# Final layer's outputs packed dense, with 3 tiles' grace and half pace, and an unread matmul in each poor tile

## The chip, the cores and the metric

The kernel runs on one core of a Trainium2 chip, in one launch. The metric is the device time of that launch in microseconds. TensorE (PE) multiplies, ScalarE (ACT) computes the exponentials, VectorE (DVE) copies, masks, normalizes and adds, GpSimd (POOL) and SyncE (SP) mostly issue DMAs. TensorE's clock is granted by a throttle; the profile lists what share of full speed was granted at each moment.

## The reference

Four attention layers with residuals: A, B, A, B. x has 2048 rows of 640, there are 32 heads of 20.

```python
def A(x, wqkv, wo):               # B is the same without the mask
    q, k, v = split(x @ wqkv)     # 32 heads, Dh = 20
    s = einsum("bhqd,bhkd->bhqk", q, k) * Dh ** -0.5
    s = where((i - j >= 0) & (i - j < 256), s, -1e9)
    return merge(softmax(s) @ v) @ wo
x = x + A(layernorm(x), A_wqkv, A_wo)
x = x + B(layernorm(x), B_wqkv, B_wo)
x = x + A(layernorm(x), A_wqkv, A_wo)
x = x + B(layernorm(x), B_wqkv, B_wo)
```

## The kernel before

**Layers, chunks, groups, units.** The layers are numbered 0 to 3; 0 and 2 have a window of 256 keys, 1 and 3 see all keys. The queries are cut into four chunks c of 512 columns, the heads into eight groups g of four. One (layer, chunk, group) is a unit; in layers 1 and 3 chunk 0 is cut further by keys (`PARTS`). The list `units` fixes the order of all units and weaves units of a windowed layer between units of a full one. The last units are those of layer 3, chunks 1 to 3, with nothing woven between.

**Tiles of the main loop.** The loop near the end of the kernel runs over tiles t. A tile is three score banks (two or four in some cases) of one unit: scores of one head for 128 keys by 512 queries, one PSUM bank each. The scores of a tile go into banks 0 to 2 for even t and 3 to 6 for odd t (`sp`), so that ACT can take the exponentials of one tile (L1284, tile `pt`) while PE writes the scores of the next (L1253). After the scores of tile t the loop calls `load_ahead()` (loads of later units on SP), `pump()` (background work, up to a credit) and `keep_clock()`, and then emits values times exponentials of an earlier tile into bank 7 (L1317). Scores use 32 rows of the array and values 21 of its columns for each head, so that four heads' matmuls run side by side.

**Order.** All of it stands under a manual schedule: each engine runs its instructions in exactly the order in which the Python code emits them. Engines wait for each other through semaphores only.

**Background tasks.** Layernorm and its transposes (`t_ln`), projections (`t_block`, `t_v`), the normalizing of a finished unit (`t_tail`) and the output projection (`t_out`) are generators. A `yield ("hold", n)` or `("pe", n)` takes n from the credit and lets the loop go on; `("wait", n)` puts the task to sleep for n tiles. `rate(t)` says how much credit a tile brings; for the tiles of layer 3, chunks 1 to 3 (`t >= len(tiles)`) it is 0.9. `take_m()` hands out one of two spare banks (5 and 6), and after an early stage bank 6 alone; `drop_m()` gives it back, from the next tile on.

**Normalizing and output.** When a unit ends, `t_tail` inverts the sums of the exponentials (L1020 to L1039), spreads them over the partitions (L1048) and multiplies (L1052) into `on[:, g, :]`. There the 80 values of a group lie as four strips of 20 rows at partitions 0, 32, 64 and 96; the other rows meet zero rows of `wop`, the output weights laid out in the same way. `t_out` therefore runs 8 matmuls over g (L541) for each of 4 x 2 blocks of 128 queries by 320 outputs, and adds the residual on DVE (L550). For the very last chunk `t_before_last` does groups 0 to 5 early (L572), and the end is left with groups 6 and 7. `load_wop` fetches the weights (four DMAs of 20 partitions, L132) whenever the next output projection belongs to the other weight matrix.

**Unread matmuls.** `unread(b)` (L620) multiplies the identity by the masks into a spare bank; nobody reads the result. `state["heat"]` counts the background and unread matmuls of a tile in units of one unread matmul, `state["carry"]` (up to 3) what earlier tiles had beyond their need, and `state["least"]` what a tile has to have: 1.76 for a tile of three banks from layer 1's first unit on, 0 from layer 3, chunk 1 on. `cool()` says that heat and carry fall short, and `keep_clock()` then first takes background work, if the credit is above -0.5, and else an unread matmul. If no spare bank is free in this tile, it stops there:

```python
            b = min(mfree, key=mfree.get)
            if mfree[b][0] > state["tick"]:
                break
            unread(b)
```

Of the kernel before, what the change touches and what calls it, by code (L numbers as in the profile page):

```python
# [12 lines left out]
ALU = mybir.AluOpType  # L13
ACT = mybir.ActivationFunctionType

P = 128
# [3 lines left out]
DH = 20  # L20
NT = S // P
KD = D // P
G = 8
C = 512
NC = S // C
EPS = 1e-5
SCALE = DH ** -0.5
HD = D // 2
# [21 lines left out]
def kernel(  # L50
# [75 lines left out]
        nc.sync.dma_start(out=x_sb[:, 4 * c : 4 * c + 4, :], in_=xin[:, 4 * c : 4 * c + 4, :])  # L126
    nc.sync.dma_start(out=wv_sb[1][:], in_=wq_view[1][:, :, 2 * D : 3 * D])

    def load_wop(w):
        v = wo_in[w].rearrange("(g j e) f -> j e g f", g=G, j=4)  # L130
        for j in range(4):
            nc.sync.dma_start(out=wop[32 * j : 32 * j + DH, :, :], in_=v[j])  # L132
# [41 lines left out]
    ready = set()  # L174
    todo = []
    tails = []
    state = {"tick": 0, "held": None, "credit": 0.0, "early": True, "act": True, "unit": 0, "heat": 0.0, "carry": 0.0, "least": 0.0}

    class Task:

# [348 lines left out]
    def t_out(l, c):  # L529
        on = ons[l, c]  # L530
        last = (l, c) == (3, NC - 1)
        while last and "before_last" not in ready:
            yield ("wait", 1)
        assert out_seq[out_n[0]] == l % 2
        for qb in range(4):
            for i in range(2):
                mb = yield from take_m()
                yp = ps[:, mb, 0:HD]
                g0 = G - 2 if last else 0
                for g in range(g0, G):  # L540
                    nc.tensor.matmul(  # L541
                        yp, lhsT=on[:, g, qb * P : (qb + 1) * P],
                        rhs=wop[:, g, i * HD : (i + 1) * HD],
                        start=(g == g0), stop=(g == G - 1),
                    )
                    if g < G - 1:
                        yield ("hold", 0.14)
                xv = x_sb[:, 4 * c + qb, i * HD : (i + 1) * HD]
                had = part_o["t"][:, 2 * qb + i, 0:HD] if last else xv
                nc.vector.tensor_tensor(out=xv, in0=had, in1=yp, op=ALU.add)  # L550
                drop_m(mb)
                yield ("pe", 0.14)
            if l < 3:
                stats(l + 1, c, qb)
            else:
                nc.sync.dma_start(out=xout[:, 4 * c + qb, :], in_=x_sb[:, 4 * c + qb, :])
        ons.pop((l, c))
        ready.add(("out", l, c))
        ready.add(("x", l + 1, c))
        n = out_n[0] = out_n[0] + 1  # L560
        if n < len(out_seq) and out_seq[n] != out_seq[n - 1]:
            load_wop(out_seq[n])

    def t_before_last():

        on = ons[3, NC - 1]
        for qb in range(4):
            for i in range(2):
                mb = yield from take_m()
                yp = ps[:, mb, 0:HD]  # L570
                for g in range(G - 2):
                    nc.tensor.matmul(  # L572
                        yp, lhsT=on[:, g, qb * P : (qb + 1) * P],
                        rhs=wop[:, g, i * HD : (i + 1) * HD],
                        start=(g == 0), stop=(g == G - 3),
                    )
                    if g < G - 3:
                        yield ("hold", 0.14)
                xv = x_sb[:, 4 * (NC - 1) + qb, i * HD : (i + 1) * HD]
                nc.vector.tensor_tensor(  # L580
                    out=part_o["t"][:, 2 * qb + i, 0:HD], in0=xv, in1=yp, op=ALU.add
                )
                drop_m(mb)
                yield ("pe", 0.14)
        ready.add("before_last")
# [27 lines left out]

    def cool():

        return state["heat"] + state["carry"] < state["least"]

    def unread(b):
# [13 lines left out]
    def keep_clock():  # L632

        while cool():
            t = choose(False)
            if t is not None and state["credit"] > -0.5:
                state["credit"] -= advance(t)
                continue
            b = min(mfree, key=mfree.get)
            if mfree[b][0] > state["tick"]:  # L640
                break
            unread(b)
        spare = state["heat"] + state["carry"] - state["least"]
        state["carry"] = min(max(spare, 0.0), 3.0)
        state["heat"] = 0.0
# [360 lines left out]
    def t_tail(l, c, g, on, oT):  # L1006
        def fill(count):

            for n in range(count * ((l, c, g) == (3, NC - 1, G - 1))):
                nc.tensor.matmul(  # L1010
                    ps[:, 0, :], lhsT=ident[:], rhs=masks[:, 0, :], start=True, stop=True
                )

        yield ("wait", 2)
        fill(2)
        mb = yield from take_m()
        warm_bank(mb)
        zp = ps[:, mb, 0:16]
        for qb in range(4):
            nc.tensor.matmul(  # L1020
                zp[:, 4 * qb : 4 * qb + 4], lhsT=oT[:, qb * P : (qb + 1) * P],
                rhs=sel4[:], start=True, stop=True,
            )
        rz = rzp.tile([P, 16], F32, name="rz", tag="rz")
        nc.vector.reciprocal(out=rz[:], in_=zp)  # L1025
        drop_m(mb)

        hl = rzp.tile([P, 2, 16], BF16, name="hl", tag="hl")
        nc.vector.tensor_copy(out=hl[:, 0, :], in_=rz[:])
        nc.vector.tensor_tensor(out=hl[:, 1, :], in0=rz[:], in1=hl[:, 0, :], op=ALU.subtract)  # L1030
        yield ("pe", 0.25)
        fill(3)
        yield ("wait", 2)
        mb = yield from take_m()
        warm_bank(mb)
        rp = ps[0:32, mb, :].bitcast(BF16)[:, 0:P]
        nc.tensor.transpose(out=rp, in_=hl[:].rearrange("p n r -> p (n r)"), identity=ident[:])
        rT = rzp.tile([32, P], BF16, name="rT", tag="rT")
        nc.vector.tensor_copy(out=rT[:], in_=rp)  # L1039
        drop_m(mb)  # L1040
        yield ("pe", 0.1)
        fill(1)
        yield ("wait", 2 if state["tick"] < last_tick[0] else 1)
        mb = yield from take_m()
        warm_bank(mb)
        zb = ps[:, mb, :]
        for qb in range(4):
            nc.tensor.matmul(  # L1048
                zb[:, qb * P : (qb + 1) * P], lhsT=spread4[:, qb, :], rhs=rT[:],
                start=True, stop=True,  # L1050
            )
        nc.vector.tensor_tensor(out=on[:, g, :], in0=oT[:], in1=zb, op=ALU.mult)  # L1052
        drop_m(mb)
        yield ("pe", 0.3)
        fill(3)
        ready.add(("tail", l, c, g))
        if (l, c, g) == (3, NC - 1, G - 3):
            push("before_last", t_before_last(), 0, 8.0)
        if g == G - 1:
            need = first_use(l + 1, c, 0) if l < 3 else len(units) + c  # L1060
            push(("out", l, c), t_out(l, c), need, 9.0)
            if l < 3:
                push_layer(l + 1, c)
    def t_zeros():

        z = ka_all[:, G : G + 4, :].rearrange("p a b -> p (a b)")
        yield ("wait", 4)
        for n in range(2):
            nc.gpsimd.dma_start(
                out=wop[:, 4 * n : 4 * n + 3, :].rearrange("p g f -> p (g f)"), in_=z[:, 0 : 3 * D]  # L1070
            )
            nc.gpsimd.dma_start(out=wop[:, 4 * n + 3, :], in_=z[:, 0:D])
            yield ("wait", 1)
        load_wop(0)
        for t in (*kts, *qts):
            nc.gpsimd.dma_start(out=t[:], in_=z[:, 0 : t.shape[1]])
            yield ("wait", 1)
        ready.add("kts")
# [67 lines left out]
    with tc.manual_schedule():  # L1146
# [49 lines left out]
        def rate(t):  # L1196

            if t >= len(tiles):
                return 0.9
            u = tiles[t][0][0]  # L1200
            if index[u.l, u.c, u.g, u.part] < woven:
                return 1.2
            done, r = 0.0, 0.6 if state["early"] else 0.3
            for task in todo:
                done += max(task.left, 0.0)
                if task.need < len(units):
                    r = max(r, done / max(starts[id(units[task.need])] - t - 16, 1))
            return min(1.1 * r, 1.0 if u.l == 0 else 0.9)
# [10 lines left out]
        while ended is None or t < ended + 8:  # L1219
# [3 lines left out]
            if t < len(tiles) or banks:  # L1223
# [23 lines left out]
                if n_b == 4:  # L1247
                    mseq[0] += 1
                    mfree[6] = (state["tick"] + 2, mseq[0])
                for n in range(2):  # L1250
                    for i, (u, j, m, b0, subs, first, last, end) in enumerate(cur):
                        for kc, q0, qn, col in subs[n : n + 1]:
# [37 lines left out]
                    pts.append((t, pt, i, b))  # L1290
                warmth = 1.76 if state["unit"] >= woven else 1.0
                state["least"] = warmth * n_b / 3 if state["unit"] < index[3, 1, 0, None] else 0.0
                load_ahead()
                r = rate(t)
                pump(r, r + 0.1)
# [98 lines left out]
```

## Time and profile before

| | us |
|---|---|
| median of 4 runs (2327.1 to 2334.91) | 2329.05 |
| the profiled execution's own time | 2327.1 |
| its span, from the first instruction to the last | 2325.4 |
| ACT busy in the span | 2176.5 |
| L1284, the exponentials (1641 of those into `pt`), busy | 2099.1 |
| PE busy in the span (matmuls) | 2011.6 |
| L541, the output projections, busy (976 matmuls) | 164.7 |
| L620, unread matmuls, busy (788) | 269.0 |
| DVE busy in the span | 1466.2 |

The busy times of one engine can be compared with the span: ACT has the least idle time. A busy matmul time is modelled and overlaps its neighbours, so a start-to-start distance is the safer price of a matmul. Layer 1, chunk 1 starts at 528.8 us, layer 3 at 1363.1 us, and layer 3's chunks 1, 2 and 3 at 1643.9, 1866.0 and 2086.5 us. Tables of windows below give, for each stretch, the busy time and number of instructions of PE, PEld (weight loads), DVE, ACT and POOL, then the mean granted clock, the share of time in which the DMA engines were busy, and GB/s.

### The profile page before, as it was taken

How to read it: one execution, taken by the hardware profiler on the slowest of the kernel's cores; microseconds unless marked ns; L12 is line 12 of the kernel's file. 1: busy time of each engine (PE TensorE's matmuls, PEld its weight loads, DVE VectorE, ACT ScalarE, POOL GpSimd, SP SyncE). 2: the span in 40 equal slices, each digit the busy share in tenths (PEclk: the TensorE clock that was granted, in tenths of full speed). 3: DMA queues.
4: the chain of work that ended last, by engine and by line, in shares of the span. 5: the costliest groups of instructions: out<-in, count | busy, mean ns of one | idle time of the engine just before them, and what ended most of it. 6: DMA issues, size and time to landing. Idle time of an engine off the chain costs nothing.

```text
span 2325.4 us, 40627 instructions
## 1 busy us (share of the span) xinstructions
PE 2011.6 (87%) x15793; PEld 724.1 (31%) x15793; DVE 1466.2 (63%) x2726; ACT 2176.5 (94%) x1751; POOL 273.8 (12%) x445
## 2 busy tenths in 40 slices
PE   8899999988889888888888898898888888888887
PEld 3344333333323332233322333342322122222222
DVE  6677775426646666666667644452677777777772
ACT  7788889999999998999999999999999999999997
POOL 4332321201100012001120012011000000000000
PEclk9999999999999999999999999999855565556556
DMA  6232322312200123102230123112200010011000
GB/s 190 82 94 75 108 69 62 91 56 65 84 19 27 47 69 94 50 14 55 76 100 29 23 84 106 37 36 71 62 29 27 27 38 27 27 38 39 28 14 12
DMA packets 84881, 132.57 MB, mean 57 GB/s; under 512 B 19760, under 2 KB 60080, under 8 KB 84688
## 3 DMA queue, kind: packets, MB, share of 16 engines
q1 hardware_dynamic: 65472, 76.80, 11.9%
q0 software_dynamic: 19216, 53.17, 7.9%
q8 instruction: 124, 2.03, 0.4%
q14 instruction: 69, 0.57, 0.1%
HBM read 98.70 MB, written 27.79 MB: 54 GB/s over the span
## 4 chain that ended last, share of the span: by engine, by line
ACT 41%; PE 27%; issue 14%; DVE 12%; DMA 1%; POOL 0%; ACTq 0%; SPq 0%; DVEq 0%; POOLq 0%
ACT pt L1284 40%; PE ps L1253 7%; PE ps L354 5%; PE ps L1317 4%; PE ps L541 4%; DVE pt L1353 3%; PE ps L455 3%; PE ps L620 2%; DVE st L304 1%; DVE on L1052 1%; ACT ka L1284 1%; DVE raw_o L887 1%; DVE oT L839 1%; PE ps L419 1%; DVE x_sb L550 1%
## 5 line engine op out<-in xcount | busy, mean ns | idle before, releaser
L1284 ACT ACTIVATE pt<-ps 128x1536 bf16<-128x1536 f32 (+2 forms) x1641 | 2099.1, 1497 | 108.6 <-PE ps L1253 102.0
L1253 PE MATMUL ps<-qt,kt 32*128 32x512 bf16 x4008 | 641.2, 455 | 192.8 <-ACT pt L1284 160.9
L1317 PE MATMUL ps<-pt,vt 128*21 128x512 bf16 x3860 | 467.3, 456 | 0.3 <-ACT pt L1284 0.3
L1253 PEld LDWEIGHTS <-kt 32*128 32x128 bf16 x4008 | 190.5, 93 | 611.1 <-issue 589.3
L1353 DVE TENSOR_TENSOR pt<-pt,masks 128x1024 bf16<-128x1024 bf16 (+5 forms) x403 | 238.1, 625 | 125.8 <-ACT pt L1284 125.3
L620 PE MATMUL ps<-masks,ident 128*128 128x512 bf16 x788 | 269.0, 394 | 27.0 <-DVE rT L1039 11.3
L354 PE MATMUL ps<-xnT,wqk 128*128 128x512 bf16 x830 | 217.6, 386 | 14.5 <-DVE on L1052 3.7
L1317 PEld LDWEIGHTS <-vt 128*21 128x21 bf16 x3960 | 99.9, 90 | 319.6 <-issue 310.6
L304 DVE CAST st<-ps 128x512 bf16<-128x512 f32 x128 | 88.4, 691 | 158.8 <-PE ps L354 158.6
L541 PE MATMUL ps<-wop,on 128*128 128x320 bf16 x976 | 164.7, 311 | 5.7 <-DVE x_sb L550 2.5
L1253 PE MATMUL ps<-qa,ka 32*128 32x384 bf16 (+2 forms) x1408 | 116.8, 276 | 30.8 <-ACT pt L1284 26.0
L887 DVE TENSOR_SCALAR xnT<-ps 128x512 int32<-128x512 f32 x88 | 60.8, 691 | 106.3 <-PE ps L880 105.9
L1052 DVE TENSOR_TENSOR on<-oT,ps 128x512 bf16<-128x512 bf16 x128 | 87.3, 682 | 57.6 <-PE ps L1048 57.1
L839 DVE CAST oT<-ps 128x512 bf16<-128x512 f32 x112 | 76.8, 685 | 73.2 <-PE ps L1317 49.0
L550 DVE TENSOR_TENSOR x_sb<-x_sb,ps 128x320 bf16<-128x320 bf16 x120 | 57.9, 483 | 97.0 <-PE ps L541 96.7
L455 PE MATMUL ps<-wv,xnT 128*128 128x320 bf16 x640 | 108.2, 301 | 10.2 <-DVE rz L1025 3.8
L541 PEld LDWEIGHTS <-on 128*128 128x128 bf16 x976 | 89.7, 100 | 69.8 <-issue 37.0
L354 PEld LDWEIGHTS <-wqk 128*128 128x128 bf16 x830 | 70.6, 98 | 108.6 <-issue 48.9
L620 PEld LDWEIGHTS <-ident 128*128 128x128 bf16 x788 | 59.1, 97 | 129.5 <-issue 127.6
L388 POOL TENSOR_SCALAR rstd<-mv 128x4 f32<-128x4 f32 x15 | 4.9, 328 | 789.5 <-DVE mv L375 789.4
L1317 PE MATMUL ps<-pt,va 128*21 128x384 bf16 (+2 forms) x1408 | 78.8, 280 | 6.8 <-DVE pt L1353 5.6
L1253 PEld LDWEIGHTS <-ka 32*128 32x128 bf16 x1408 | 44.3, 92 | 98.0 <-issue 88.9
(107 smaller groups left out, 1796.0 us busy)
## 6 DMA issues: line engine op xcount, KB each, us to landing
vt<-v_d SPq DMA_DIRECT2D x48, 336.0 KB
kt<-k_d SPq DMA_DIRECT2D x192, 80.0 KB
wqk<-in_B_wqkv_dram POOLq DMA_DIRECT2D x80, 160.0 KB, 3.8
wqk<-in_A_wqkv_dram POOLq DMA_DIRECT2D x70, 160.0 KB, 3.4
k_d<-st POOLq DMA_DIRECT2D x75, 128.0 KB, 2.2
q_d<-st POOLq DMA_DIRECT2D x75, 128.0 KB, 2.2
qt<-q_d SPq DMA_DIRECT2D x384, 20.0 KB
v_d<-vs POOLq DMA_DIRECT2D x16, 336.0 KB, 3.0
```

The lines of the kernel that those rows point to most:

```text
L304: nc.vector.tensor_copy(out=out_, in_=in_)
L354: nc.tensor.matmul(pq, lhsT=wt[:, dc, :], rhs=xt[:, dc, :], start=(dc == 0), stop=(dc == KD - 1),)
L455: nc.tensor.matmul(pv, lhsT=xt[:, dc, i * P : (i + 1) * P], rhs=wv_sb[l % 2][:, dc, h * HD : (h + 1) * HD], start=(dc == 0), stop=(dc == K ...
L541: nc.tensor.matmul(yp, lhsT=on[:, g, qb * P : (qb + 1) * P], rhs=wop[:, g, i * HD : (i + 1) * HD], start=(g == g0), stop=(g == G - 1),)
L620: nc.tensor.matmul(ps[:, b, :], lhsT=ident[:], rhs=masks[:, 0, :], start=True, stop=True)
L839: nc.vector.tensor_copy(out=oT[:], in_=op)
L887: V.tensor_scalar(out=xi.bitcast(I32)[:, i * C : (i + 1) * C], in0=side["psum"], scalar1=SCALE * LOG2E * E23, scalar2=127.0 * E23, op0=ALU ...
L1052: nc.vector.tensor_tensor(out=on[:, g, :], in0=oT[:], in1=zb, op=ALU.mult)
L1253: nc.tensor.matmul(sp[:, i, col * P : (col + qn) * P], lhsT=u.k(kc, j), rhs=u.q(j, q0, qn), start=True, stop=True,)
L1284: nc.scalar.activation(out=pt[:, i:k, b0 * P :], in_=sp[:, i:k, b0 * P :], func=ACT.Exp, scale=SCALE,)
L1317: nc.tensor.matmul(op[32 * j : 32 * j + VW, q0 * P : (q0 + qn) * P], lhsT=u.v(kc, j), rhs=pg[:, i, col * P : (col + qn) * P], start=(first ...
L1353: nc.vector.tensor_tensor(out=pt_[:, i:k, b0 * P :], in0=pt_[:, i:k, b0 * P :], in1=mv_, op=ALU.mult,)
```

## The change

It has two parts.

**Outputs of layer 3.** For layer 3 (`packed`), except for groups 6 and 7 of the last chunk, `t_tail` writes the product into one of three staging slots, `on[:, 5 + g % 3, :]`. Two tiles later it issues short copies on SP's queue that move the four strips of 20 rows to dense places: row r of the 640 goes to partition r % 128 of `on[:, r // 128, :]`. A strip that crosses a multiple of 128 takes two copies. After the last group of a chunk (and after group 5 of the last chunk) the task sleeps three more tiles before the output projection may start. `t_out` then runs 5 matmuls of 128 rows for each block in place of 8, and `t_before_last` 4 in place of 6. `load_wop` gets a dense form: one DMA of 128 partitions for all of it and four for the strips of groups 6 and 7; it is called once, when the outputs of layer 2 are done. `rate(t)` gives 0.45 in place of 0.9 in layer 3, chunks 1 to 3.

**Unread matmuls.** From layer 1, chunk 1 on, until layer 3, chunk 1, a tile whose own heat is under 0.9 counts as cool even if the carry covers its need. And after the early stage, where the spare bank is taken, `keep_clock` no longer stops: it notes an unread matmul as owed, and the next tile puts it on PE ahead of its scores, into the first of its score banks, which the scores then overwrite.

```diff
+    def packed(l, c):
+        return l > 2
...
+    def load_wop(w, dense):
+        if dense:
+            nc.sync.dma_start(out=wop[:, 0:KD, :], in_=wo_in[w].rearrange("(b p) f -> p b f", p=P))
+            if w and out_n[0] == 12:
+                v = wo_in[w].rearrange("(g j e) f -> j e g f", g=G, j=4)
+                for j in range(4):
+                    nc.sync.dma_start(
+                        out=wop[32 * j : 32 * j + DH, G - 2 : G, :], in_=v[j][:, G - 2 : G, :]
+                    )
+            return
...
     def t_out(l, c):
...
+        dense = packed(l, c) and not last
+        a, b = (0, KD) if dense else (G - 2 if last else 0, G)
...
-                g0 = G - 2 if last else 0
-                for g in range(g0, G):
+                for g in range(a, b):
...
     def t_before_last():
...
-                for g in range(G - 2):
+                for b in range(4):
+                    n = min(P, (G - 2) * 80 - b * P)
                     nc.tensor.matmul(
-                        yp, lhsT=on[:, g, qb * P : (qb + 1) * P],
-                        rhs=wop[:, g, i * HD : (i + 1) * HD],
-                        start=(g == 0), stop=(g == G - 3),
+                        yp, lhsT=on[0:n, b, qb * P : (qb + 1) * P],
+                        rhs=wop[0:n, b, i * HD : (i + 1) * HD],
+                        start=(b == 0), stop=(b == 3),
                     )
...
     def cool():
+        if state["least"] > 0.0 and state["heat"] < state["floor"]:
+            return True
         return state["heat"] + state["carry"] < state["least"]
...
             b = min(mfree, key=mfree.get)
-            if mfree[b][0] > state["tick"]:
+            if state["early"] and mfree[b][0] > state["tick"]:
                 break
-            unread(b)
+            if mfree[b][0] > state["tick"] - (0 if state["early"] else 0):
+                state["owed"] += 1
+                state["heat"] += 1.0
+            else:
+                unread(b)
...
     def t_tail(l, c, g, on, oT):
...
-        nc.vector.tensor_tensor(out=on[:, g, :], in0=oT[:], in1=zb, op=ALU.mult)
+        end = (l, c) == (3, NC - 1) and g >= G - 2
+        spread = packed(l, c) and not end
+        nu = on[:, 5 + g % 3 if spread else g, :]
+        nc.vector.tensor_tensor(out=nu, in0=oT[:], in1=zb, op=ALU.mult)
         drop_m(mb)
         yield ("pe", 0.3)
         fill(3)
+        if spread:
+            yield ("wait", 2)
+            for j in range(4):
+                r, a = (4 * g + j) * DH, 0
+                while a < DH:
+                    b, o = divmod(r + a, P)
+                    n = min(DH - a, P - o)
+                    nc.sync.dma_start(
+                        out=on[o : o + n, b, :], in_=nu[32 * j + a : 32 * j + a + n, :]
+                    )
+                    a += n
+            if g == G - 1 or (l, c, g) == (3, NC - 1, G - 3):
+                yield ("wait", 3)
...
         def rate(t):
             if t >= len(tiles):
-                return 0.9
+                return 0.45
...
+                while state["owed"]:
+                    state["owed"] -= 1
+                    nc.tensor.matmul(
+                        sp[:, 0, :], lhsT=ident[:], rhs=masks[:, 0, :], start=True, stop=True
+                    )
                 for n in range(2):
                     for i, (u, j, m, b0, subs, first, last, end) in enumerate(cur):
...
                 state["least"] = warmth * n_b / 3 if state["unit"] < index[3, 1, 0, None] else 0.0
+                state["floor"] = 0.9 if state["unit"] >= index[1, 1, 0, None] else 0.0
```

More of the change, by code (lines that the diff above doesn't have):

```diff
@@ L127 @@
     nc.sync.dma_start(out=wv_sb[1][:], in_=wq_view[1][:, :, 2 * D : 3 * D])
-    def load_wop(w):
+    def packed(l, c):
[10 more added lines that the diff above has]
+            return
         v = wo_in[w].rearrange("(g j e) f -> j e g f", g=G, j=4)
@@ L176 @@
     tails = []
-    state = {"tick": 0, "held": None, "credit": 0.0, "early": True, "act": True, "unit": 0, "heat": 0.0, "carry": 0.0, "least": 0.0}
+    state = {"tick": 0, "held": None, "credit": 0.0, "early": True, "act": True, "unit": 0, "heat": 0.0, "carry": 0.0, "least": 0.0, "floor": 0.0, "owed": 0}
     class Task:
@@ L543, in t_out @@
                         rhs=wop[:, g, i * HD : (i + 1) * HD],
-                        start=(g == g0), stop=(g == G - 1),
+                        start=(g == a), stop=(g == b - 1),
                     )
-                    if g < G - 1:
+                    if g < b - 1:
                         yield ("hold", 0.14)
@@ L560, in t_out @@
         n = out_n[0] = out_n[0] + 1
-        if n < len(out_seq) and out_seq[n] != out_seq[n - 1]:
-            load_wop(out_seq[n])
+        if n < len(out_seq) and (n == 12 or out_seq[n] != out_seq[n - 1]):
+            load_wop(out_seq[n], n >= 12)
     def t_before_last():
@@ L570, in t_before_last @@
                 yp = ps[:, mb, 0:HD]
-                for g in range(G - 2):
+                for b in range(4):
+                    n = min(P, (G - 2) * 80 - b * P)
                     nc.tensor.matmul(
-                        yp, lhsT=on[:, g, qb * P : (qb + 1) * P],
-                        rhs=wop[:, g, i * HD : (i + 1) * HD],
-                        start=(g == 0), stop=(g == G - 3),
+                        yp, lhsT=on[0:n, b, qb * P : (qb + 1) * P],
+                        rhs=wop[0:n, b, i * HD : (i + 1) * HD],
+                        start=(b == 0), stop=(b == 3),
                     )
-                    if g < G - 3:
+                    if b < 3:
                         yield ("hold", 0.14)
@@ L1073, in t_zeros @@
             yield ("wait", 1)
-        load_wop(0)
+        load_wop(0, False)
         for t in (*kts, *qts):
```

## The prediction, made before the changed kernel ran

> **What bounds the kernel now.** I read the page first, then windows of the last layer, then the neighbourhoods in which the granted clock falls, then the order of work on PE.
>
> ```profile
> span 2325.4 us, 40627 instructions
> ...
> PE 2011.6 (87%) x15793; PEld 724.1 (31%) x15793; DVE 1466.2 (63%) x2726; ACT 2176.5 (94%) x1751; POOL 273.8 (12%) x445
> ...
> PEclk9999999999999999999999999999855565556556
> ```
>
> ACT is busy for 94% of the span, so a saving counts only where ACT stands idle (some 149 us). The clock row shows two regimes: nearly full until about 1640 us, then half for most of the final layer.
>
> ```profile
> 1644.00:1690.00 46.00, 38.69 (x274) 15.01 (x273) 34.31 (x56) 41.30 (x31) 0.00 (x0) 0.73 0.15 48
> 1690.00:1880.00 190.00, 156.98 (x969) 38.78 (x966) 143.84 (x205) 190.00 (x140) 0.00 (x0) 0.50 0.10 29
> 1880.00:1910.00 30.00, 25.70 (x193) 10.52 (x189) 22.09 (x36) 25.33 (x19) 0.00 (x0) 0.84 0.15 48
> ...
> 2100.00:2130.00 30.00, 27.47 (x198) 11.01 (x197) 23.97 (x38) 25.76 (x20) 0.00 (x0) 0.80 0.15 48
> ...
> 2262.00:2284.00 22.00, 18.38 (x135) 7.51 (x131) 8.23 (x15) 18.65 (x14) 0.00 (x0) 0.81 0.00 1
> ```
>
> Columns: stretch, length, busy time of PE, PEld, DVE, ACT, POOL, then the clock. Between 1690 and 1880 ACT never idles, at half clock. It idles only where an output projection is woven in: 4.70, 4.67, 4.24 and 3.35 us, together 17.0 us. That is all the first part of the change can win.
>
> ```profile
> 560.00:580.00 20.00, 15.91 (x112) 6.14 (x110) 15.52 (x29) 15.61 (x12) 6.89 (x10) 0.74 0.46 113
> 660.00:680.00 20.00, 18.17 (x150) 5.85 (x147) 16.45 (x37) 18.47 (x20) 0.00 (x0) 0.88 0.19 56
> 680.00:700.00 20.00, 18.10 (x119) 5.19 (x119) 4.75 (x6) 18.33 (x14) 0.00 (x0) 0.86 0.00 0
> 840.00:860.00 20.00, 18.39 (x148) 7.93 (x147) 12.11 (x22) 17.84 (x14) 2.89 (x7) 0.85 0.25 45
> 900.00:920.00 20.00, 16.92 (x139) 5.46 (x139) 15.87 (x34) 17.53 (x14) 3.37 (x5) 0.83 0.24 69
> 980.00:1000.00 20.00, 17.68 (x167) 5.98 (x163) 16.83 (x35) 19.47 (x16) 0.00 (x0) 0.91 0.04 14
> 1120.00:1140.00 20.00, 19.41 (x149) 8.01 (x148) 11.80 (x22) 17.61 (x14) 0.00 (x0) 0.86 0.10 18
> 1180.00:1200.00 20.00, 15.93 (x138) 5.69 (x138) 16.61 (x32) 17.94 (x14) 3.40 (x5) 0.91 0.28 81
> ```
>
> These are all the dips of the clock between 528 us (layer 1, chunk 1) and 1643 us: in these 160 us ACT idles 17.2 us, in the other 955 us of that stretch 25.3 us, or 0.53 per 20 us. The 3.4 us ahead of five dips hold one to three unread matmuls (1, 3, 1, 1, 1); an undisturbed 3.4 us at 650 holds five.
>
> **Final layer, outputs.** Three chunks lose 3 of 8 matmuls in 8 blocks (72), the piece before the last loses 2 of 6 in 8 (16). The order of the changed kernel puts the outputs of a chunk into 8 tiles of 5 (groups of 3, 1, 1, 2, 1; 3, 1, 3, 1; 3, 1, 2, 1, 1) and the piece into 5 and 3 tiles of 4, where before single tiles took 8 or 6. The price of a tile is read here:
>
> ```profile
> 1881.06 0.61 PE L1253 MATMUL ps<-qt,kt 32*128 32x512 bf16 x3
> 1882.11 2.29 PE L541 MATMUL ps<-wop,on 128*128 128x320 bf16 x8 [0.45 <-DVE on L1052]
> 1884.34 0.61 PE L1317 MATMUL ps<-pt,vt 128*21 128x512 bf16 x4
> 1884.88 0.61 PE L1253 MATMUL ps<-qt,kt 32*128 32x512 bf16 x3
> 1885.42 1.99 PE L541 MATMUL ps<-wop,on 128*128 128x320 bf16 x8
> ```
>
> At half clock 8 outputs take 1884.34 - 1882.11 = 2.23 us, 0.279 each; values and scores 0.54 each, start to start. ACT needs 1.33 us a tile (seven start between 1907.79 and 1917.10). So a tile with 5 outputs costs PE 1.08 + 1.40 = 2.48, 1.15 over ACT; one with 4 costs 2.20, 0.87 over. The first tile of the burst above took PE 3.82 and ACT then idled 1.91, so 0.58 of an excess stays unseen. The clock came back 4.3, 4.9, 3.2 and 5.2 us after a burst's first output (by the clock in 2 us windows), 4.4 on average: 1.8 tiles of five or 2.0 of four. At full clock an output takes 0.149 (8 in 1.19 us, 1887.99 to 1889.18) and five fit beside 0.66 of scores and values in 1.33.
>
> If the clock rises as before: a cold group of five costs 1.77 x 1.15 - 0.58 = 1.45; three first groups 4.4; three second groups, half of them still at full clock (the full stretches lasted 10 to 20 us, the second groups come 10 to 16 us later), 2.2; three late singles at 0.57, half cold, 0.9; the piece 2.0 x 0.87 - 0.58 = 1.2 and half of 3 x 0.87 - 0.58, 1.0. Sum 9.7 in place of 17.0: 7.3 gained. If it does not rise at all: four groups of three at 2.87, two pairs at 1.72, eight singles at 0.57, the piece 3.77 + 2.03, together 25.3: 8.3 lost. Five outputs are 1.40 of 2.48 us of a tile (56%), against 1.67 of 2.75 (61%) with six, which still raised the clock. That is nearer the first end; I take a gain of 6.
>
> A page of the Trainium skill, "TensorE: Matmul & The Clock Gate" (section "What's actually happening"), holds that the clock halves after an idle window of about 3.4 us and returns after a busy one. The rows differ on the first half: in 671.8 to 675.2 PE was busy 2.28 of 3.40 us and the clock still fell at 675. By that rule only a stretch in which PE stands, as before 569, would bring a dip, the added matmuls would cure none, and the middle would gain nothing.
>
> **Moves.** 135 short copies in SBUF join SP's queue, four to six per head group. Issuing a copy of 20 rows there takes 0.33 us, so 45 us over the last 680; the queue otherwise waits (593 us on PE at one line alone). Behind a move that waits for DVE's multiply stand the next unit's loads (9 issues, 3 us), due a whole unit of 20 tiles, 27 us, later. The landing of SP's copies is not shown; the nearest rows are 2.2 us (k_d<-st) and 6.6 (qt<-ka, 128 rows). In chunk 2 the multiply ends at 2096.8, four issues end at 2098.1, landing 2100.3 at 2.2 us; the first output is at 2102.25: hidden with 1.9 to spare. At 6.6 PE stands 2.5 us with the next scores behind it, there and before the piece: 2 x (2.5 - 0.58) = 3.8 lost. I take 2.2 (a transfer of similar size) and nothing. The dense load of wop stands where the four old loads stood, a chunk before its first reader. Two four-bank tiles fewer are worth nothing: 1.76 us (1917.10 to 1918.86) against 4/3 of 1.33.
>
> **Unread matmuls.** By the order, 110 go into the next score bank and 31 more into the spare, 141 of 512 columns at 0.149 x 512/320 = 0.24 us: 34 us of PE, of which most lies in tiles where PE waits for ACT anyway. One in the score bank waits, as the scores behind it do, until ACT has released that bank; ACT then has a whole tile of 1.33 us in hand, so the 0.24 shows only where PE is already 0.58 late. 27 of the tiles with one at their head also carry four or more projection or output matmuls; if half of those are past the 0.58, 27 x 0.24 / 2 = 3.2 lost; none, 0; all, 6.5. Cured, by what the order puts ahead of them: 675 (two more), 839 and 1119 (value projections between the layernorm's tiles), 993 (two), 1194 (two), one of 904 and 911. Not 569: PE waits there for the normed rows. From the rows that is 3.2 + 2.2 + 2.4 + 0.5 + 2.1 + 1.2 = 11.6, less 6.5 x 0.53 that such stretches lose anyway, 8.2. The shifted order leaves thin stretches near 877 and 908, each worth a dip of some 1 us: 2. Net 8.2 - 2 - 3.2 = 3 gained; between 8.2 gained and 6.5 + 2 lost.
>
> **Sum.** -6 - 3 = -9 against the profiled execution's 2327.1 us (span 2325.4 and 1.7 around it). The median of the runs shown is 1.95 above that, so 2329.05 - 9 = 2320.
>
> **The rivals.**
> A, the crowd: the unread matmuls cure nothing and cost 3.2, while the outputs gain 4 to 6. For it: a quarter of them head loaded tiles; against it: the dips follow the counts of unread matmuls. 2329 + 3 - 5 = 2327.
> B, the other side: groups of five stay at half clock, so every output tile pays 1.15. Place: the four output bursts. It decides when the clock is not back within three tiles of a chunk's first output. For it: 56% is thinner than anything that raised the clock here; against it: PE is saturated then, as it was four times out of four. +8.3, with the middle at 0 to +3: about 2338.
> C: the moves land late, PE stands before chunk 2 and the piece: 2320 + 3.8 + the lost head start, about 2325.
>
> **How the numbers follow.** My forecast 0.55, A 0.25, B 0.14, C 0.06. Bounds of the forecast: the outputs between -8 and -3, the middle between -8 and +3, so 2313 to 2329; A reaches 2323 to 2331, B to 2340. The range 2311 to 2332 leaves out most of B and a little of the rest. A change under 0.3% (7 us) can't be told from none here: faster means under 2322. The forecast gives 0.47 of faster and 0.08 of same; A 0.03, 0.2 and 0.02; B all slower but 0.03; C 0.02 and 0.04. So 0.52, 0.35, 0.13.
>
> **What would show it.** Right: ACT's idle time in the four output stretches falls from 17.0 to about 10 us, with a rise of the clock at each; dips between 528 and 1643 fall from eight to three or four, the one near 569 staying; the pace elsewhere is unchanged. Wrong: output tiles in rows at 0.50 with ACT idle about 1 us in each (B); dips gone but idle time before scores grown in tiles with projections (A); an output matmul waiting for a DMA (C).

## The result, and the profile after

The changed kernel takes 2323.15 us (median of 44 runs, 2314.03 to 2333.18), the kernel before 2329.34 (65 runs beside them): ratio 0.9973, 95% interval 0.9966 to 0.9981, or 6.2 us (4.4 to 7.9). The forecast was 9. Single executions of one kernel lie up to 10 us from its median, the slower ones at a lower mean granted clock (0.858 in the slowest of the changed kernel, 0.867 in the fastest), and the profiled execution of the changed kernel is one of its slower ones (2328.2 us). So the two profiles are compared stage by stage, not by their spans.

The page of the changed kernel:

```profile
span 2326.4 us, 40950 instructions
...
PE 2044.4 (88%) x15846; PEld 719.4 (31%) x15846; DVE 1464.5 (63%) x2726; ACT 2180.4 (94%) x1752; POOL 271.5 (12%) x445
...
PEclk9899999999999999999999999999755555556556
```

PE is busy 33 us longer, with 53 matmuls more (141 unread ones added, 88 outputs dropped). ACT's share is the same.

The windows of its output stretches (columns as before: stretch, length, busy time of PE, PEld, DVE, ACT, POOL, granted clock):

```profile
1654.00:1700.00 46.00, 39.26 (x248) 12.86 (x247) 34.79 (x54) 43.41 (x33) 0.00 (x0) 0.60 0.18 52
1700.00:1704.00 4.00, 2.59 (x28) 0.80 (x26) 2.55 (x5) 3.33 (x4) 0.00 (x0) 0.93 0.13 45
1704.00:1890.00 186.00, 155.00 (x955) 38.44 (x954) 142.14 (x204) 185.93 (x136) 0.00 (x0) 0.50 0.12 33
1890.00:1932.00 42.00, 34.33 (x227) 11.07 (x223) 32.38 (x49) 39.15 (x30) 0.00 (x0) 0.70 0.11 34
...
2110.00:2152.00 42.00, 35.78 (x236) 10.03 (x238) 31.54 (x48) 39.23 (x29) 0.00 (x0) 0.66 0.12 36
...
2270.00:2292.00 22.00, 18.23 (x139) 6.45 (x136) 6.83 (x14) 21.29 (x17) 0.00 (x0) 0.81 0.02 4
```

ACT's idle time in them is 2.59 + 0.67 + 2.85 + 2.77 + 0.71 = 9.6 us, in place of 17.0. Between these stretches it idles 1.2 us more (0.5 before), so the whole last stage, up to the last exponential, has 10.8 in place of 17.5. The clock is over 0.5 in each stretch, so it still came back.

And the windows in which the clock dips now, between layer 1, chunk 1 (529.9 us) and layer 3, chunk 1 (1653.9 us), with one that no longer dips:

```profile
570.00:590.00 20.00, 19.13 (x139) 7.69 (x139) 11.55 (x20) 16.96 (x12) 1.04 (x4) 0.83 0.28 45
660.00:680.00 20.00, 18.25 (x162) 6.65 (x161) 16.99 (x39) 19.07 (x21) 0.00 (x0) 1.00 0.20 55
...
900.00:920.00 20.00, 17.81 (x132) 5.46 (x129) 14.83 (x27) 16.72 (x13) 3.39 (x5) 0.83 0.21 62
...
1180.00:1200.00 20.00, 17.86 (x155) 5.75 (x153) 16.81 (x35) 17.59 (x14) 3.40 (x5) 0.79 0.31 92
1200.00:1220.00 20.00, 18.01 (x131) 5.85 (x128) 7.29 (x10) 18.65 (x15) 2.18 (x4) 0.95 0.12 38
1260.00:1280.00 20.00, 17.55 (x169) 5.84 (x168) 16.33 (x33) 18.54 (x15) 0.00 (x0) 0.91 0.13 39
```

Five dips stand in place of eight (the one near 1192 reaches over two windows). Yet that stretch takes 1124.0 us here against 1115.2 before, while the rest, from layer 3, chunk 1 to the end, takes 672.4 against 681.5. In these two executions the gain is all in the last stage.

### The profile page after: what moved, and what is told of

Its sections match the earlier page's. It is cut to its first block, busy times and chain, and to the rows that moved or that the text cites. A ratio compares the mean times of both kernels' runs of the same rounds, so it can differ in the third digit from the quotient of the medians.

```text
span 2326.4 us, 40950 instructions
## 1 busy us (share of the span) xinstructions
PE 2044.4 (88%) x15846; PEld 719.4 (31%) x15846; DVE 1464.5 (63%) x2726; ACT 2180.4 (94%) x1752; POOL 271.5 (12%) x445
## 4 chain that ended last, share of the span: by engine, by line
ACT 40%; PE 28%; issue 15%; DVE 11%; DMA 0%; POOL 0%; SPq 0%; ACTq 0%; DVEq 0%; POOLq 0%
ACT pt L1326 39%; PE ps L1295 7%; PE ps L367 5%; PE ps L1360 4%; PE ps L555 4%; PE ps L468 3%; DVE pt L1396 2%; PE ps L637 2%; DVE st L317 1%; ACT ka L1326 1%; DVE raw_o L908 1%; DVE on L1076 1%; DVE oT L860 1%; DVE x_sb L564 1%; PE ps L1289 1%
## 5 line engine op out<-in xcount | busy, mean ns | idle before, releaser
L1295 PEld LDWEIGHTS <-kt 32*128 32x128 bf16 x4008 | 182.6, 93 | 586.2 <-issue 569.0
L637 PE MATMUL ps<-masks,ident 128*128 128x512 bf16 x819 | 288.1, 393 | 36.9 <-DVE on L1076 7.6
L637 PEld LDWEIGHTS <-ident 128*128 128x128 bf16 x819 | 64.9, 97 | 141.4 <-issue 139.4
L555 PEld LDWEIGHTS <-on 128*128 128x128 bf16 x904 | 81.0, 100 | 73.0 <-issue 44.7
```

The lines of the kernel that those rows point to most:

```text
L555: nc.tensor.matmul(yp, lhsT=on[:, g, qb * P : (qb + 1) * P], rhs=wop[:, g, i * HD : (i + 1) * HD], start=(g == a), stop=(g == b - 1),)
L637: nc.tensor.matmul(ps[:, b, :], lhsT=ident[:], rhs=masks[:, 0, :], start=True, stop=True)
L1295: nc.tensor.matmul(sp[:, i, col * P : (col + qn) * P], lhsT=u.k(kc, j), rhs=u.q(j, q0, qn), start=True, stop=True,)
```

## The experiments

Stage lengths are read from the traces by the start of the first exponential of a unit: "middle" runs from layer 1, chunk 1 to layer 3, chunk 1, "last" from there to the end; one execution each. "Half" is the time at half clock in the middle. Ratios are to the kernel before, run beside each.

| kernel | median us | ratio (95%) | middle | half | last |
|---|---|---|---|---|---|
| before | 2329.34 | 1 | 1115.2 | 47.8 | 681.5 |
| changed | 2323.15 | 0.9973 (0.9966 to 0.9981) | 1124.0 | 27.3 | 672.4 |
| e1_outputs | 2321.37 | 0.9968 (0.9954 to 0.9982) | 1118.2 | 54.6 | 671.4 |
| e2_unread | 2335.68 | 1.0027 (1.0013 to 1.0042) | 1128.3 | 44.4 | 683.3 |
| e3_full_pace | 2325.29 | 0.9984 (0.9971 to 0.9996) | 1116.1 | 3.4 | 672.6 |
| e4_pace_alone | 2323.99 | 0.9983 (0.9972 to 0.9995) | 1115.1 | 47.8 | 681.6 |
| e5_floor_alone | 2322.95 | 0.9974 (0.9964 to 0.9985) | 1119.7 | 34.8 | 673.4 |
| e6_owed_alone | 2320.26 | 0.9969 (0.9959 to 0.9980) | 1116.6 | 23.9 | 670.8 |
| e7_no_pull | 2330.95 | 1.0010 (0.9997 to 1.0022) | 1131.4 | 27.3 | 672.5 |
| e8_split | 2317.77 | 0.9953 (0.9937 to 0.9970) | 1116.0 | 44.4 | 671.9 |
| e9_ln_later | 2324.67 | 0.9980 (0.9966 to 0.9994) | 1126.9 | 47.8 | 670.3 |
| e10_owed_twice | 2326.87 | 0.9984 (0.9973 to 0.9994) | 1124.0 | 13.7 | 672.9 |
| e11_no_grace | 2331.28 | 1.0004 (0.9987 to 1.0021) | 1117.1 | 6.8 | 677.7 |
| e12_split_owed | 2318.74 | 0.9950 (0.9934 to 0.9966) | 1121.6 | 37.5 | 671.9 |

The kernels of e1 to e4 ran beside a kernel before of 2329.11 us, e5 to e8 beside one of 2328.98, e9 to e12 beside one of 2331.40.

**Each part alone.** e1 takes the floor and the owed matmuls out of the changed kernel; e2 puts them alone into the kernel before.

```diff
     def cool():
-        if state["least"] > 0.0 and state["heat"] < state["floor"]:
-            return True
...
-            if state["early"] and mfree[b][0] > state["tick"]:
-                break
-            if mfree[b][0] > state["tick"] - (0 if state["early"] else 0):
-                state["owed"] += 1
-                state["heat"] += 1.0
-            else:
-                unread(b)
+            if mfree[b][0] > state["tick"]:
+                break
+            unread(b)
```

> The outputs of the final layer alone: packed dense, 3 tiles' grace, half pace; no unread matmul is added. Theory M (the outputs carry the whole gain, the unread matmuls cancel out): 6 us under the kernel before, ratio 0.9974, ACT idle in the four output stretches down from 17 to about 10 us. Rival N (both parts gain, as predicted): 3 to 4 us under, 0.9985. Rival K (the unread matmuls cost): 8 or more under, 0.9965.

> The unread matmuls alone on the kernel before: outputs sparse at the old pace. M: the kernel before within 1.5 us. N: 2.5 to 3.5 us under it, 0.9987. K: 2 or more over it. In the profile, N wants fewer than eight dips of the clock between 528 and 1643 us with the idle time of ACT down from 42; K wants fewer dips and the idle time up.

Alone the outputs gain 7.5 us (4 to 11), alone the unread matmuls lose 6.3 (3 to 10). Rival K, which expected the unread matmuls to cost, fits both; M fits the first alone, and the predicted N neither. The two don't add up to the changed kernel: their sum is a gain of 1.2 us, and it has 6.2. So inside it the price of the unread matmuls is less sure: it lies 1.8 us over e1, within both intervals.

In e2's profile the price can be seen in one place, three windows around a dip:

```profile
1255.00:1259.00 4.00, 2.75 (x35) 1.01 (x29) 3.66 (x9) 4.00 (x4) 0.00 (x0) 1.00 0.54 168
1259.00:1283.00 24.00, 23.06 (x141) 5.57 (x142) 14.55 (x29) 17.56 (x13) 0.00 (x0) 0.50 0.01 4
1283.00:1287.00 4.00, 3.73 (x30) 1.32 (x31) 3.22 (x4) 3.47 (x3) 0.00 (x0) 1.00 0.00 0
```

PE's order within it, with unread matmuls into the spare bank (L622) and into the score bank (L1258):

```profile
1268.70 0.61 PE L1258 MATMUL ps<-masks,ident 128*128 128x512 bf16 x1
1269.24 0.61 PE L1264 MATMUL ps<-qt,kt 32*128 32x512 bf16 x3
1269.78 0.61 PE L622 MATMUL ps<-masks,ident 128*128 128x512 bf16 x1
```

Here the clock stays at half for 24 us, longer than any dip of the kernel before in that stage (10 us), with PE busy throughout and ACT idle for 6.4. An unread matmul takes 0.54 us, start to start, at half clock, so the work meant to bring the clock back makes PE late behind ACT meanwhile. One or two such matmuls a tile did not bring it back for seven of the 3.4 us steps in which it changes.

**The pace.** e3 sets the changed kernel's 0.45 back to 0.9, e4 sets 0.45 in the kernel before.

> The changed kernel with the pace 0.9 in place of 0.45. If the half pace is what gains (a burst spread out): 4 us or more over the changed kernel, output stretches at 15 us of idle ACT. If the packing gains by itself (fewer matmuls): within 2 us of the changed kernel. If the half pace only makes more cold groups: 2 or more under the changed kernel.

> The kernel before with the pace 0.45 in place of 0.9 and nothing else: sparse outputs of 8 matmuls a block, at half pace. If the pace gains by itself: 3 or more us under the kernel before. If eight in a tile stay too many at half clock whatever lies between (2.23 + 1.08 us of PE against 1.33 of ACT): no gain, or 2 to 4 us over it, as more of the blocks then fall at half clock.

The last stage takes 672.6 us at the full pace with packed outputs, 681.6 at half pace with sparse ones: the packing gains by itself, and the pace moves nothing there. ACT idles 10.8 us in that stage at either pace with packed outputs. By the times, e3 is 2.1 us over the changed kernel and e4 4 under the kernel before by the ratio, clear of no change and not explained by its profile, in which neither middle nor last is shorter. What the pace is worth stays open within some 4 us.

**Floor, owed, and the pull.** The theory was that the floor does harm by pulling projections together. e5 has the floor alone on the new outputs, e6 the owed matmuls alone; e7 has both, but a tile that is cool by the floor alone takes only an unread matmul:

```diff
     def keep_clock():
...
-            if t is not None and state["credit"] > -0.5:
+            short = state["heat"] + state["carry"] < state["least"]
+            if t is not None and state["credit"] > -0.5 and short:
```

> The changed kernel without the owed matmuls: a tile still counts as cool under 0.9, but where the spare bank is taken nothing is put into the next score bank. Theory P (the floor costs, because a tile under it first pulls background work forward, so projections stand in denser runs): as slow as the changed kernel or up to 3 us slower, 2323 to 2326. Theory O (an unread matmul at the head of a tile that carries a projection costs): faster than the outputs alone by 2 or more, 2317 to 2319. If the dips that are cured simply balance either: 2321, as the outputs alone.

> The changed kernel without the floor: need and carry decide as before, only the owed matmuls are added (115 of them, 38 fewer into the spare). P: no pull, so 2317 to 2320, with fewer dips than the outputs alone and no added idle time. O: 2323 to 2326.

> The changed kernel, but a tile that is cool by the floor alone takes no background work, only an unread matmul (869 into the spare, 108 owed). P: 3 to 5 us under the changed kernel, 2318 to 2320. O: the changed kernel within 1.5 us, or slower, as there are 48 more unread matmuls.

The theory fell: without the pull the kernel is 7.8 us slower than with it, with 48 more unread matmuls. e5 and e6 can't be told from e1. To see the price without the dips, the middle was cut into 55 pieces of 15 exponentials, and in each only executions were used that no dip touches. Kernels with the same middle (before, e1, e4, e8; changed, e2, e3, e11) were taken together, the shortest of each set. 51 pieces can be compared: 1014.1 us without the added matmuls, 1023.0 with them, **8.9 us more** (with the cuts at other places, 7 to 11). With the owed ones alone it is 5.3 more over 47 pieces, with the floor alone 3.8 over 46, in e7 14.8 over 49. For the 141 matmuls added in the changed kernel, the 77 in e6 and the 189 in e7 that is 0.06 to 0.08 us each: what costs is added work on PE, whichever way a tile comes by it. A version with the owed matmul behind the scores of its tile was not tried.

**The owed matmuls doubled.** e10 issues each of e6's 115 twice.

```diff
-                    nc.tensor.matmul(
-                        sp[:, 0, :], lhsT=ident[:], rhs=masks[:, 0, :], start=True, stop=True
-                    )
+                    for _ in range(2):
+                        nc.tensor.matmul(
+                            sp[:, 0, :], lhsT=ident[:], rhs=masks[:, 0, :], start=True, stop=True
+                        )
```

> The owed matmuls alone on the new outputs (e6_owed_alone), each of the 115 issued twice. If an added matmul at the head of a tile is hidden by ACT unless PE is already late (my prediction: half of the 27 loaded tiles at 0.24 us each): 2320 to 2324. If its cost is what ate the gain of the cured dips (the middle without dips about 3 us longer with 115 of them): 3 to 5 us over e6_owed_alone, 2323.5 to 2325.5. If at half clock they hold PE behind ACT and lengthen the dips: more than 6 over it, with a dip of over 12 us in the profile.

3.5 us slower by the ratios (0.9969 and 0.9984, their intervals overlap), the middle 1124.0 against 1116.6, although it spends 10 us less at half clock. The dip-free pieces (49) are 16.0 us longer than without added matmuls, against 5.3 in e6 (115 owed, but 38 fewer into the spare): 115 more cost 10.7 us, or 0.09 each of the 0.24 that one takes. So about a third of added PE work shows, not nothing, as the second expectation has it. No dip over 12 us stands in the middle, so the last of the three is not met.

**The grace.** e11 takes the three tiles' sleep out of the changed kernel (`("wait", 3)` becomes `("wait", 0)`).

> The changed kernel without the three tiles' grace after the last move of a chunk. If the moves land late (four or five issues of 0.72 us, as the profile of the changed kernel has them, then the landing): an output matmul waits 1 to 3 us for a DMA before chunk 1's and the piece's first block, ACT idle 1 to 5 us more, 2324 to 2328. If they land in time even so: the changed kernel within 1.5 us.

The changed kernel's whole gain is gone (1.0004), more than the 1 to 5 us expected. The waits of PE in its profile (line, what for, total us, times, longest):

```profile
PE ps L555 <- DMA on<-on: 4.0, 2, 2.3
...
PE ps L587 <- DMA on<-on: 2.6, 1, 2.6
```

In the changed kernel no output matmul waits for a DMA. One chunk of e11, its multiply, SP's four moves behind it, and the first output that waits:

```profile
1655.69 0.68 DVE L1076 TENSOR_TENSOR on<-oT,ps 128x512 bf16<-128x512 bf16 x1
```

```profile
1656.40 2.97 SPq L1087 DMA_DIRECT2D on<-on  x4
```

```profile
1660.76 0.43 PE L555 MATMUL ps<-wop,on 128*128 128x320 bf16 x1 [1.71 <-DMA on<-on]
```

```profile
L1087 SPq DMA_DIRECT2D on<-on x135: 554/717/839, 1607.1 to 2262.4; - x135
```

The last line gives the time of one issue, least, median and most, in ns: 0.72 us, where a load from DRAM on the same queue takes 0.33. From the end of the multiply (1656.37) to the output that may start it is 4.4 us. The last stage is 5.3 us longer than in the changed kernel; the rest of the loss is not seen in this profile, which is e11's fastest execution.

**Outputs cut over three tiles.** e8 is e1 with each dense block as 2, 2 and 1 matmuls in three tiles, and three tiles of rest.

```diff
-                    if g < b - 1:
+                    if dense and g in (1, 3):
+                        yield ("pe", 0.14)
+                        yield ("wait", 1)
+                    elif g < b - 1:
                         yield ("hold", 0.14)
...
                 drop_m(mb)
                 yield ("pe", 0.14)
+                if dense:
+                    yield ("wait", 3)
```

> The outputs alone, with each dense block of five cut over three tiles as 2, 2 and 1 matmuls, the bank held meanwhile, and three tiles of rest after it. If it is the excess of one tile over ACT at half clock that costs (5 outputs: 1.15 us; 2 outputs: 1.08 + 0.56 - 1.33 = 0.31, under the 0.58 that stays unseen): idle time of ACT in the three chunks falls from 8.4 us (profile of the outputs alone: 2.4, 3.3, 2.7) to under 2, time 6 us under the outputs alone, 2315; the clock then stays at half throughout the three chunks. If holding the only spare bank delays the side exponentials or the tails instead: idle time appears elsewhere in the chunks, and 2321 or more.

Its chunks, in windows:

```profile
1648.00:1690.00 42.00, 36.55 (x221) 9.65 (x220) 32.89 (x51) 41.73 (x32) 0.00 (x0) 0.50 0.16 46
1690.00:1860.00 170.00, 147.12 (x885) 34.50 (x881) 126.59 (x185) 168.36 (x124) 0.00 (x0) 0.51 0.12 34
1860.00:2085.00 225.00, 193.27 (x1163) 45.84 (x1159) 174.70 (x252) 222.25 (x164) 0.00 (x0) 0.50 0.11 34
2085.00:2270.00 185.00, 164.69 (x978) 38.21 (x975) 142.10 (x207) 183.93 (x135) 0.00 (x0) 0.50 0.11 32
```

The clock stays at half, as expected, and the idle time is spread thin, not gone: 0.27 + 1.64 + 2.75 + 1.07 = 5.7 us here, where under 2 was expected, and 7.7 in the whole last stage against 9.6 in e1. The last stage is as long as e1's (671.9 and 671.4). The median is the lowest of all (2317.77, 6 runs); against e1 the intervals overlap, and since the stage that was changed is no shorter in the profile, the gain over e1 is not shown to be the split's.

**The layernorm later.** e9 is e8 with `("wait", 2)` after the inverse deviation made 4, and `("wait", 1)` after the first normed rows made 2.

> The split outputs (e8_split), and in the layernorm task two more tiles between the inverse deviation on POOL and its first use, and one more before the first transpose; no added unread matmuls. If the dips near 569, 839 and 1119 us come from PE standing at these transposes: 2 to 4 us under e8_split, 2314 to 2316, and those three dips gone. If they come from too little dense work around there, whatever PE waits for: same dips, 2317 to 2319.

Neither. Of the three dips one (now at 560) is shorter and two are gone, but others come at 1297, 1328, 1356 and 1397; the middle is 10.9 us longer than e8's, while the stage ahead of it is 8.3 shorter (521.8 against 530.1). Later layernorms help the early layers and delay the later ones in these two executions; a version that waits longer in the early layers alone was not tried.

**Both together.** e12 has e8's split and e6's owed matmuls.

> The split outputs of e8_split together with the owed matmuls of e6_owed_alone. If their gains over the outputs alone (3.6 and 1.1 us by the medians) are both real: 2316 to 2317. If the owed matmuls only shift dips: 2318, as e8_split.

2318.74 us, 0.9950 of the kernel before run beside it: as e8. With e8 it is the best version here by ratio, both clearly faster than the kernel before; against the changed kernel (0.9966 to 0.9981) e12's interval just touches and e8's overlaps, so that they beat it is likely and not shown.

## Why the prediction was right, and where it was not

**The outputs: right in mechanism and near in size.** Forecast: idle time from 17.0 to 9.7; measured 9.6. The burst of five, PE's order in the changed kernel:

```profile
1675.10 1.51 PE L555 MATMUL ps<-wop,on 128*128 128x320 bf16 x5
1676.55 0.61 PE L1295 MATMUL ps<-qt,kt 32*128 32x512 bf16 x3
1677.19 1.49 PE L555 MATMUL ps<-wop,on 128*128 128x320 bf16 x5
...
1679.16 0.61 PE L1295 MATMUL ps<-qt,kt 32*128 32x512 bf16 x3
```

```profile
1679.88 2.96 ACT L1326 ACTIVATE pt<-ps 128x1536 bf16<-128x1536 f32 x2 [1.16 <-PE ps L1295]
```

Five outputs take 1.45 us and a tile with values 2.61 from score to score (2.48 forecast); this group cost ACT 0.07 + 1.16 + 0.06 = 1.29 us (1.45 forecast), and the clock was back 4.8 us after its first output (4.4 forecast). The taken value, 6, was a lean towards rival B that the runs did not need: the last stage is 8.1 to 10.7 us shorter in all seven kernels with dense, uncut outputs and the grace (changed, e1, e3, e5, e6, e7, e10). In the changed kernel it is 9.1: 6.7 is ACT's idle time over the whole stage, 0.8 is ACT's busy time, and 1.6, which the sum had at nothing, lies after the last exponential (13.0 us before, 11.4 in the changed kernel); in e5 and e10, with the same order of tiles, it is 13.0 again, so it is not shown to come from the change.

**Rival B fell:** the clock came back in every output stretch with five to a tile. **Rival C fell, but by less than the prediction had it.** The row for an issue was the wrong one: 0.72 us in place of 0.33. From multiply to output 4.4 us are needed where 3.5 were summed, so of the 5.5 us available in chunk 2 (by the trace of before) some 1 was to spare, not 1.9. e11 shows C's price where the grace is missing: PE waits in the first block of chunks 0 and 1 and of the piece, and not in that of chunk 2, which comes 5.5 us after its multiply.

**The unread matmuls: wrong in sign.** The step that failed is "Net 8.2 - 2 - 3.2 = 3 gained". Its list of cures was mostly right: the dips near 675, 839, 993 and 1119 are gone, the one near 569 stays, two near 904 and 912 remain where one was expected, the one near 1194 stays and is longer (10 us). The dips near 839 and 1119 stand in all four profiles without the added matmuls and in none of the four with them (675: in three of four, and in none); the one near 569 is gone in e3 and e11. But the crowd is 8.9 us, not 3.2, by the dip-free pieces. The sum charged only tiles with an owed matmul and four or more projection or output matmuls. Yet 4.4 of the 8.9 us lie in the 25 pieces with 20 or more of these, 2.9 in the 17 that hold none, and 1.6 in the other 9. One such place without them, in the changed kernel, is where a unit ends:

```profile
990.28 0.38 PE L637 MATMUL ps<-masks,ident 128*128 128x512 bf16 x1 [0.90 <-DVE rT L1060]
...
991.00 0.39 PE L1289 MATMUL ps<-masks,ident 128*128 128x512 bf16 x1
991.32 0.39 PE L1295 MATMUL ps<-qt,kt 32*128 32x512 bf16 x3
```

```profile
991.82 1.45 ACT L1326 ACTIVATE pt<-ps 128x1536 bf16<-128x1536 f32 x1 [0.31 <-PE ps L1295]
```

The normalizing holds the spare bank, PE has just waited 0.90 us for its step on DVE, the owed matmul then puts the scores off by 0.32, and ACT idles 0.31. A matmul becomes owed only where the spare bank is in use, and at such a place PE can be late already, so that the slack that was to cover half of the loaded tiles is spent. That this accounts for all of the 8.9 us is not shown.

And fewer dips bought less than 6.2. Over the four profiles with each middle the mean length is 1121.4 us with the added matmuls (1116.1 to 1128.3) and 1116.1 without (1115.1 to 1118.2), 5.3 more, so the dips saved about 8.9 - 5.3 = 3.6, although the time at half clock fell from 48.7 to 20.5 us on average. e3 and e11 show the limit: they have 3.4 and 6.8 us of half clock left in the middle, and it takes 1116.1 and 1117.1, no less than without the added matmuls. Nearly all dips cured only pays for the work that cures them. Rival A named this crowd as a loss of 3.2 with nothing cured; its place was half right and its price too low.

That the sum came out near is in part luck, as the two errors oppose each other: 3 us more from the outputs, some 8 less from the middle (5.3 lost for 3 gained). These stage readings add to 9.1 - 5.3 = 3.8 us of gain where the times have 6.2 (4.4 to 7.9); they rest on one execution of each kernel, and the rest is left open. The page of the Trainium skill that the prediction weighed, "TensorE: Matmul & The Clock Gate" (section "What's actually happening"), would have had the middle gain nothing; the middle lost, but by work on PE and not for the page's reason: denser work did remove the dips near 839 and 1119, ahead of which PE had been busy 2.02 and 1.80 of 3.40 us.

## What to carry to other kernels

Before work is added to an engine that is off the critical path, sum it over the stretches in which that engine is already late, by its own work or by a wait, not over the whole span: its idle share elsewhere covers nothing there. A dummy matmul that keeps the clock up has its own price, here 0.06 to 0.09 us of the 0.24 that it takes in stretches without a dip, and it takes 0.54 at half clock. And a move through a DMA between producer and consumer needs its own measured issue time in the margin; without the few tiles' grace the whole gain was gone.

## What was not expected of the hardware

- An issue of a copy from SBUF to SBUF of 20 rows of 1 KB takes 0.72 us on SP's queue (135 of them, 0.55 to 0.84), a load of 20 such rows from DRAM 0.33.
- The clock stayed at half for 24 us with PE busy 23.06 of 24.00, in a stretch with one or two dense matmuls a tile (e2, 1259 to 1283); five outputs a tile brought it back in 4.8.
- With 28 us less of half clock in the middle its dips saved only about 4 us: a dip costs what PE is late by, and in most of a dip ACT still has work. Pieces with a dip, each against the shortest of its set, sum to at least 10.6 us a profile without the added matmuls (48.7 us of half clock) and to 6.8 with them (20.5).
